# The first key tile and the rotation table brought and rotated in two parts, three small loads begun by another engine

## The chip, the cores and the metric

The kernel runs on one core of a Trainium2 chip. Its engines are TensorE (PE, with PEld for its weight loads), VectorE (DVE), ScalarE (ACT), GpSimd (POOL) and SyncE (SP), which here does nothing but issue transfers. Sixteen DMA engines move the data. The metric is the device time of one execution in microseconds (us): 590.54 us as the median of three runs before the change, 590.2 the fastest, 591.32 the slowest.

## The reference

Attention with rotary positions, then a two-layer perceptron with a squared ReLU. Batch 4, 8 heads, 576 positions, head size 64; the width is 512, the inner width 2048.

```python
def rotate(x):
    x1, x2 = x[..., :32], x[..., 32:]
    return concatenate([x1 * cos - x2 * sin, x1 * sin + x2 * cos], axis=-1)
scores = matmul(rotate(q), rotate(k).T) / 8
attn = exp(scores - max(scores)); attn = attn / (sum(attn) + 1e-9)
x = matmul(attn, v)                      # heads joined: 2304 x 512
r = maximum(x @ w_in, 0)
out = (s * (r * r) + b) @ w_out          # s and b are single numbers
```

## The kernel before

Heads are handled in 16 pairs; pairs 0 to 3 are the first batch. Of a pair, `st_k`, `st_q` and `st_v` hold 128 partitions by 9 (or 10) tiles of 64 numbers. Each k and q is loaded (L529), multiplied with the table and summed in three steps on DVE or POOL: `z` = x times the sines (L588), x = x times the cosines (L590), x = x + `z` (L592). For pairs 0 to 3, k and q are then turned by PE with the identity, four 128x128 transposes (L766) and two 64x64 pieces (L769), into one of two PSUM tiles named `s`; ACT copies the result into `qkT` (L412). From `qkT`, PE computes the scores of two row tiles at a time (L653) into both `s` tiles; DVE takes the row maxima `nm` (L678), and ACT the exponentials `p` (L412), after which the `s` tile is free again. Some of the `p` tiles are turned by PE with a diagonal matrix `dg` made from the identity (L794, L796).

Beside this, 32 blocks of the two weight matrices, 512 KB each, arrive as `x` (L440), are rebuilt by ACT (two passes, L412; POOL or DVE does some of them) and DVE (`wio<-x,wio`, L409), and PE forms a product of each with itself (L493) to find a bound of their size. From about 60 us the perceptron runs between the attention of later pairs, and PE has work of one kind or another to the end.

What every engine does next is written out: `plan` builds the list of pieces, `ORDER` says in which order they are emitted, `PICKS` which engine takes a piece that could go to several, `SLOTS` which buffer it uses. All loads go through SP's queue, in that order; an issue waits when its buffer or its completion semaphore (eight in turn) is not free. The rotation table `tab` (432 KB) is the first load, the identity `ident` (64 KB) the second, the k of pair 0 the third. The two scalars, `sb`, are loaded between the weights, and nine small DVE steps (`sb_scale`) use them later.

Of the kernel before, what the change touches and what calls it, by code (L numbers as in the profile page):

```python
# [42 lines left out]
    "BwKXEDJzEUJcJ0J2BYBxJ8EhKDJ9BdByBiKEBMBHCGCVCHKUKbJ-J1J_CIKAKFD8J3BNCbKGBjKeEIEVD9KcJqJ4B1KfALJ5KYKdEBJrKBK5B2KVKgJ6B3CX"
    "BzKhEQaaCWKiEHK6KHCKaZCYCcacD-CdB_K7abCeKlERCQB4KqadB5KjaeKZKrafKmakKsCLKkKtEKLfKIKaKnCAK8CMalLgKuFVCNELanKvCBEMC2ENKwb0"
    "LhEOamK9EPCCK-KxEEavB6aoLFapESCSKyEWKoCRLSEYayKJK0LGKpaqCTaxLHK1KCCOagC4EXC3CxawK_LTC5ahB8EZCgB7CJLCLULiCPEkLVB9LZEiKKLI"
    "LWLDaiKLKzLJLab1ajazb2b3K2LXLEarLjb4EqLKLra0Eab5a1Erb6asLkLLLsEjatLPL4CmLtElb7K3LMEtMFK4LbLNChCibGLQLAL5MGbJCzEmCjLBMHbI"
    "EnEuMIbHL6Llb8LYL7EoLoEsL_b9bKLOauCyEpEvEwbLLpLRa9bMEyLua8L8MAE6b-a7E5EzLvCra6b_FULqE7Exa2LwcAMJC0MOa-cBMKLxL9LcL1a_MUcC"
    "MLCoLybRMPEcL-MVL2bSE9cDMBbTMQLzE8bUFHL3cEFEMRbVcFL0bWbNFFcGFILnLea3LdcHMWE-CkMea4LmcICnMXMSMfCZMYCUbOEbcJMTCpa5MgcKE0MZ"
    "CfCtM0CaFGMbMhMlMCMiM1CsM6M2ClMjMrMEMaMDMcFXCDCuM7B-MkbeMsbACEbccLM8MtMMM9MmE_bPMuNBFAFhMNM3cMFBFJM-MnbdFCcNFDNCFMbfcOMd"
    "M4bBbgFKNEM5FTbCFNE1bXC6FibDNFM_EdC1NGNibhcPNfFYGINjMocQMvFLNkcRMwbENHNgNDcSNLMqMxNUMpbQNINANMNhbqNJFWMyEebpbiFeNVbnNlNN"  # L50
    "NmC7NWFjNRFfboNnNKNSCqNobrCvNvMzNTFgbYNwNqbZFOCwNxcaNrN9NXbscTbaGLNYN-cbNcNybtNOccNZNzcUN_cdNdGVOANPNecVbbdAOBcWbjFPN0ce"
    "dBbkNaN1FQcfdCblNbNQN2cXOCN6dDFZbmcYdEFRdFE2ODbudGOEdHFadIFbN3dJNsbvdKFcdLcZdMbwFdGWNpcgONdNFmbxE3FkchOQdPFnciFlbydOOFcj"
    "FoOOckdZdQN7dRcldYdSOGcmdTdidacndbFpN4djcoOPOROIFtPJcpdkNtbFPKcqOSE4dUOTPLOHOJdWFSPMdlOeN5dccrObNudVGXFqOKdsOUOcOYcsddOd"
    "d3N8ctOVOfcuFwd2GjOZdmFuFrOWOgdtF4d4FvdnOrd5bzOucvOhdeOiOscwOmdXOjOvOLcxOncydgOaPNOtF5dfOwOkdhOod6czO8OMdpc0O9duOXO5FxF6"
    "drdvc1eBOlPOO6c2O-eAGJc3dwGHPPc4PSdxOxeCeUd7O7Oyc5eVO2O_eDPAPTFyPEPVO3c6OpF7PBPWOzPFPUdoO4Oqdqc7PXdzPCPGc8eWdyO0PYeXPgF8"
    "PDGMFzd1Phd9F0FsPiO1PjF9eLeEPZPkPaF1QIPleFPdeKGKQJPmPeQLeMd_F2PnPbeNPrd0QMPHeOPsPoc9QNd8PtePQKd-F3PpF-c-P6PfeGQOGAP7eIPI"
    "c_PqP9ehF_eHP8GBGNeJPceQeieYQPejQTeSP-PQGmQwGOQQeZekeRPRP_eleTemGPenQRQAeaGCeoQBecQxQFebepGQQyeqGRederesGhQGetPxQZPyQCPu"
    "euPzGDGaQUewPwGSPvQHQaevQDQbQSGTQzQcefQlQVQ0P0exe5P1eyGUeeQEP2Qme6Q1P3GYfNezP4e7Qde0QeQ2QnQiP5fOe8QjQ3GbGiQ4e1GZfPG8e3Q7"
    "QfRKGcfDe9Q8Qke-fEfQQ5QoGEQpRLQtRBfFGFQqQWRMRCfGQufRQre_GlQ9RNRDGve2QhfSe4GwRbfHQsROfYGkREfIQYRPQ6fXGsRQRFGeGtRYQvQXRRGx"
    "fBRVRSRZfJfZQgfLRcRafARTfaG7fCG9RGGGegRsRdGnfiHxGoGpRWReGdG_RHfbfhGqGrRfRtG0Q-fjRjRgRkRuRhRpfkRXfKG-RqfMGuRJRrR6HGfsGyG4"  # L60
    "RIR7RAHAfrHJRvR8RlHKfTfcftRifVGzfuSVG1fURURwSWfdRxR0R3RySXG2ffR4fvHBfWR1feR5G5HCSYHDR9fwQ_fgHER-HFSKSZHVSCRmHwR_SLSaG3fl"
    "fmf2RnHHgCHIf1RogDHMSAfngEf3SBSDSHSbf4HLgFfpf5R2SIfoHOHzfqgGSJgHRzScfygIgJSdgKf6f0SMSEgLfxHPSNfzHSgMHNf7GfSggNgOf8SoHQgP"
    "f-f9ShgASlH0HWgQSmf_HvHYSegRSnGgG6SFgSSOSpgTSPgUgbSGSfHgSSHhSqS2HRgaSrSsSTSwSiS3Szgcg5StS0gdSUSQgegkHyHiSRHZgVg4S4H6HTHj"
    "S1glSxILS5HXS6TRS7gmTUTSS-gngWTVTTgXgZgfgoThS8g6Sjg7TiTWSuTXguHkS9TjS_IOTGTYHlTATZgvgpSkH9THSygYHUggTIH-SvTDHaghTEgwgiTa"
    "gxgqH_gyHbTtTFhMTuTcTJTKH7TOgjTLTkHcgrHdHeTqHfTlTdHoHmgtTrTvTBTMTmTPUJTCTbhNTsUKTwgzg8TNT4ULHphCT5TQUMg9T7hDTeTxT8TyT1g1"
    "hEIKT2g3TnT6g_HnhFgsT9Tzg0HqUVT-hGT_g2UWUATfhOUNhHUXUBhPUxUDT0INg-UETghAUyTohjUSH8hXhkUFUTUOhBhlUCUPhJhQhWUUhRTpIXUYUghY"
    "hmhIT3hnhZhLhoUZUhhaUdhTIjUahphqHrhKhbUihSUbUzgBhVhrhshtUjhuU0hvU1H1VIUkU2hdH2U3UlUGVJUmUeVZH3UIUnUcUrVKhUVahcUfH4hwVbVL"
    "heUHVcUsUoURU6hfImVMh7UtH5U7VNIAUph8ICUqVOU9VPVdh9VeiaU-UQh-VTHsVfiZIlh_IBU_hyVQIJU8VRHtibhxIuicVAIYVzIvhzUuV0hhh0VBhgh1"
    "VUVFWBU5iFUvWCVCU4IZUwV1iGIDWDVSVDViIMh2VwVEiQWEVxVGVyiPVViAiHVjiIVlVHiRh4IUV2h6VkWFVmIkIPiCIEV3WGV4iEIViSWNiJh3IWh5WHiB"
    "iKiTiDVniUiMIQV5WYVoiLIwVWIRIFWZISITV7IgWOiuIoV6VpV8VtWaVqiOInV9IciWIaVrWKWPVgitIxidIdIGVhWbiviNWciwiVVuWdiXIyVvijWLWeVs"  # L70
# [16 lines left out]
    "SSSSSSGSSSGGGVGGVGGVSGVGSSSSSGSSVVSSVVSSVVSSVVSSGSGSVGGSGVVGGSVVGSSGVSSSVGGSSGVSGSVVGGSVVSGSVVGSSVGSVSVVSGSVVSGSSGSSSSSG"  # L87
    "SGSVGSGSSSSSSSGSSSGSSGSSSGSGSSGVGGSSSSGSSSSSSGSSGSSSSSSSSSSGGSSSSSGVSSSSGSSSSSGSSGSSSSGVSGSSSSGSSGSGSVGSSSVSSSGSSGSSGSGG"
    "SGSSSSVGGSGGSGSSSGSSSGVSSVSVSSGSSVVGVSSVVGSGVVGSSVVVSSGVSSVVSSGVVVVVVGSSGVSSVGGSGVSVSVGGSGSVSSVSSSGVSGVVSGSSSSSSSSSSGSSS"
    "SSSGSSGSGSGSSSGSGGSGGSGGSSGSVSSSSSSSSSVSVSVSSSSVSSSSVVVSSSSSSSSSGSVSVSSSVSVSGSVVSVVVVSVSVVSVSVSSSSSSGSVVVVVVSSSVSVVVSSVV"  # L90
# [3 lines left out]
SLOTS = (
    "000111230101000001010102003011110011011011222130001310002013113020010103100110000101010011223012310100010101110112001121"
    "103011230030310011001334132500100100013001101031100103011003110514021013101021300130001132105200000111320114100310000121"
    "010001100320153112000310020110002111034100121041310113050011210000114200012331301002110103000031110233401012200001211021"
    "153011211110011032111201412211000320100520112110000113301202010200111310502001032011001300001011100011301140113020202121"
    "051020030002011110120121110003011120023501012001313014101111241000013020120101021225313201300011001030100110341200111310"
# [1001 lines left out]
```

## Time and profile before

| what | before |
|---|---|
| median of three runs | 590.54 us |
| the profiled execution | 591.62 us |
| its span from first to last instruction | 589.8 us |
| PE busy | 570.6 us, 97% of the span |
| DVE busy | 464.0 us, 79% |
| ACT busy | 417.1 us, 71% |
| POOL busy | 117.7 us, 20% |

The profiled execution is 1.82 us longer than its span: that much lies around the instructions. It is 1.08 us above the median of the runs. A row of a timeline gives the start, the duration, engine, line, operation, output from inputs, and in brackets the idle time of the engine before it and what ended it; rows of the same kind that follow each other are merged with a count.

### The profile page before, as it was taken

The numbers are of one execution on the slowest core, as the hardware profiler recorded it, in microseconds if no ns is written. First come the engines' busy times: TensorE is split into PE (matmuls) and PEld (weight loads), VectorE is DVE, ScalarE is ACT, GpSimd is POOL, SyncE is SP. The second block draws the span as 40 slices with busy tenths as digits, with TensorE's granted clock in tenths as the row PEclk, the third lists the DMA queues.
The fourth block names the chain that finished last, engine by engine and source line by source line (L and its number), as shares of the span: only waits on it lengthen the run. The fifth ranks groups of instructions, "written<-read, shape, count | busy, mean of one in ns | idle before, by whom it ended". The sixth has DMA issues, their size and how long they took to land.

```text
span 589.8 us, 12277 instructions
## 1 busy us (share of the span) xinstructions
PE 570.6 (97%) x4621; PEld 389.3 (66%) x4621; DVE 464.0 (79%) x975; ACT 417.1 (71%) x869; POOL 117.7 (20%) x123
## 2 busy tenths in 40 slices
...
PEclk9999999999999999999999999999999999999999
...
GB/s 300 345 299 297 243 256 214 191 184 151 155 203 156 122 180 169 222 193 185 168 105 167 186 147 148 151 169 143 101 102 21 82 93 84 57 61 1 37 1 36
DMA packets 210011, 90.32 MB, mean 153 GB/s; under 512 B 192288, under 2 KB 196768, under 8 KB 209952
## 3 DMA queue, kind: packets, MB, share of 16 engines
...
q14 instruction: 23, 0.19, 0.1%
...
## 4 chain that ended last, share of the span: by engine, by line
PE 91%; DVE 3%; DMA 2%; ACT 2%; issue 1%; SPq 0%; DVEq 0%
PE px L889 29%; PE po L972 27%; PE px L759 9%; PE s L671 8%; PE px L922 4%; PE po L943 4%; PE s L653 3%; PE s L972 2%; DMA st_k<-in_k_dram 2%; PE po L794 1%; PE s L672 1%; PE px L493 1%; PE px L813 1%; DMA pt<-pab 1%; PE s L660 1%
## 5 line engine op out<-in xcount | busy, mean ns | idle before, releaser
L889 PE MATMUL px<-xa,wio 128*128 128x256 f16 x1536 | 179.7, 273 | 0.0
L972 PE MATMUL po<-wio,g 128*128 128x512 f16 x720 | 171.4, 379 | 0.8 <-ACT o L412 0.8
L889 PEld LDWEIGHTS <-wio 128*128 128x128 f16 x1536 | 147.7, 98 | 28.6 <-issue 2.0
L412 ACT ACTIVATE p<-s,nm 128x576 f32<-128x576 f32 x144 | 105.4, 733 | 36.0 <-DVE s L680 23.1
L972 PEld LDWEIGHTS <-g 128*128 128x128 f16 x816 | 75.8, 98 | 74.0 <-issue 3.4
L409 DVE SCALAR_TENSOR_TENSOR pab<-p,sum,pab 128x576 f16<-128x576 f32 x136 | 114.0, 849 | 7.6 <-ACT pab L412 3.7
L680 DVE TENSOR_SCALAR_CACHE_REDUCE s<-s,sc 128x576 f32<-128x576 f32 x108 | 87.9, 818 | 16.8 <-PE s L672 15.7
L406 POOL TENSOR_SCALAR pab<-p,sum 128x576 f16<-128x576 f32 x54 | 48.1, 894 | 240.5 <-DVE sum L708 189.7
L412 ACT ACTIVATE hr<-px,xc 128x512 f32<-128x512 f32 x64 | 43.7, 682 | 52.4 <-PE px L889 52.3
L913 DVE SCALAR_TENSOR_TENSOR g<-hr,xc,g 128x512 f16<-128x512 f32 x64 | 48.4, 761 | 18.8 <-ACT g L412 18.1
L412 ACT ACTIVATE pab<-p,sum 128x576 f16<-128x576 f32 x64 | 48.7, 767 | 11.0 <-DVE sum L708 10.4
L404 DVE TENSOR_SCALAR g<-hr,xc 128x512 f16<-128x512 f32 x24 | 11.9, 497 | 47.9 <-ACT hr L412 32.6
L759 PE MATMUL px<-pt,v 128*64 128x320 f16 (+2 forms) x640 | 48.9, 281 | 0.3 <-DMA pt<-pab 0.2
L412 ACT ACTIVATE hr<-hr 128x512 f32<-128x512 f32 x68 | 42.7, 628 | 1.5
L671 PE MATMUL s<-qkT 128*128 128x512 f16 (+1 forms) x120 | 41.4, 383 | 0.1
L671 PE MATMUL s<-kS,qkT 128*128 128x512 f16 (+1 forms) x120 | 41.3, 380 | 0.0
L412 ACT ACTIVATE g<-hr,xc 128x512 f16<-128x512 f32 x40 | 28.7, 717 | 16.9 <-PE po L972 10.9
L759 PEld LDWEIGHTS <-v 128*64 128x64 f16 x640 | 32.1, 110 | 11.1 <-issue 7.4
L671 PEld LDWEIGHTS <-qkT 128*128 128x128 f16 (+1 forms) x240 | 22.5, 100 | 22.8 <-issue 3.7
L922 PE MATMUL px<-x,wio 128*128 128x128 f32 x256 | 31.4, 278 | 0.0
L922 PEld LDWEIGHTS px<-x,wio 128*128 128x128 f32 x256 | 29.8, 192 | 2.2 <-issue 1.2
L412 ACT ACTIVATION_READ_ACCUMULATOR p<-s,nm 128x1 f32 x144 | 28.2, 196 | 0.0
(154 smaller groups left out, 796.3 us busy)
## 6 DMA issues: line engine op xcount, KB each, us to landing
...
```

The costliest lines, as they stand in the source:

```text
L406: eng.tensor_scalar(out=out, in0=in0, scalar1=s1, scalar2=s2, op0=op0, op1=op1)
L409: nc.vector.scalar_tensor_tensor(out=out, in0=in0, scalar=scalar, in1=in1, op0=op0, op1=op1)
L412: nc.scalar.activation(out=out, in_=in_, func=func, **kw)
L653: nc.tensor.matmul(ps[h][:, to], d["qF"][hh, t * P:(t + 1) * P], d["kF"][hh, keys], start=True, stop=True)
L671: nc.tensor.matmul(ps[rows, MAIN:2 * MAIN], lhs, kk[:, h:8:2], start=(n == 0), stop=(n == 1))
L680: nc.vector.tensor_scalar(out=T["s"], in0=T["s"], scalar1=st[pr]["es"], scalar2=None, op0=ALU.mult, op1=ALU.min, accum_out=T["nm"])
L759: nc.tensor.matmul(o[64 * h:64 * h + 64, c], v_rows(pr, h, k, z), p_rows(pr, 2 * (i // 4) + h)[:, k, c], start=((z, k) == todo[0]), stop=( ...
L889: nc.tensor.matmul(ph, w16[0][:, f, wz, cc], X["xa"][:, xz, c], start=(c == 0 and n == 0), stop=(c == NC - 1 and n == 2))
L913: nc.vector.scalar_tensor_tensor(out=g[:, 1], in0=r, scalar=xs[u]["c"][:, 2:3], in1=g[:, 0], op0=ALU.add, op1=ALU.subtract)
L922: nc.tensor.matmul(ph, wi[:, f + 1, c * P:(c + 1) * P], xs[0]["x"][:, c, j * P:(j + 1) * P], start=(c == 0), stop=(c == NC - 1))
L943: nc.tensor.matmul(X["po"][:, j * DM:(j + 1) * DM], gs["h", j, f - f % 4][:, f % 4 * P:(f % 4 + 1) * P], wo[:, f + 1], start=(n == 1), sto ...
L972: nc.tensor.matmul(po, g[:, gz, jj], w16[1][:, f, wz, to], start=(n == 1 and i == 0), stop=(n == NF and i == 2))
```

## The change

The table is loaded in two parts, tiles 0 to 3 and tiles 4 to 8, and so is the k of pair 0; the loads alternate (table, k, table, k) at the head of SP's queue. The rotation of that k runs as two pieces of three steps each, one for each part, and the first part is given to POOL. The identity and the two scalars are no longer pieces of the plan: ACT's queue issues them before its first instruction. The order, the engines of many pieces and the buffers are written out anew for the whole program.

```diff
 ORDER = (
-    "AAC8C9A9AMDYDZAXAyDADBDDDCA_DEDGA-DFANBADIDKAODcA4DHAPBBDJDdAiI9DLDfDMAYDeAZI-A0AaAzDgAnI_A1JFJADiARA5DOA6DhJGDmA7AkDkJB"
+    "AAC7ABC8C9A8DbALDcAWAxDADBDDDCDEDGDFDHA9DJA-DIDfDLDKDNA_ANDgA3DMDODiAMDPJADhAXAOAYJBAhJIAzAyAZJJDjAaAQJCDlA0JDA4DkAmA5DR"
...
         for nm in "kqv":
-            add(DMA, "load_x", pr, nm, w=[(nm, pr)])
+            if pr == 0 and nm == "k":
+                for i in range(2):
+                    add(DMA, "load_h", pr, nm, i, p=[(nm, pr)], w=[("half", i)])
+            else:
+                add(DMA, "load_x", pr, nm, w=[(nm, pr)])
...
         for nm in "kq":
-            add((DVE, POOL), "rotate", pr, nm, steps=3, r=[("tab",)], w=[(nm, pr), ("z", pr, nm)])
+            if pr == 0 and nm == "k":
+                for i in range(2):
+                    add((DVE, POOL), "rot_half", pr, nm, i, steps=3, r=[("tab", i)], w=[("half", i)], p=[(nm, pr), ("z", pr, nm)])
+            else:
+                add((DVE, POOL), "rotate", pr, nm, steps=3, r=[("tab", 0), ("tab", 1)], w=[(nm, pr), ("z", pr, nm)])
...
-    add(DMA, "load_tab", w=[("tab",)])
     for i in range(2):
-        add(DMA, "load_sb", i, p=[("sb",)])
-    add(DVE, "sb_scale", steps=9, r=[("sb",)], w=[("sc0",)])
+        add(DMA, "load_tab", i, w=[("tab", i)])
+    add(DVE, "sb_scale", steps=9, w=[("sc0",)])
...
-    def load_tab():
-        nc.sync.dma_start(out=tab, in_=rope)
-        nc.sync.dma_start(out=ident, in_=eye)
...
+    def cut(i):
+        return slice(4 * i, 4 + 5 * i)
+
+    def load_h(pr, nm, i):
+        if not i:
+            st[pr][nm] = new(stage, nm, [P, 9, D], F32, "st_" + nm)
+        nc.sync.dma_start(out=st[pr][nm][:, cut(i)], in_=src_of[nm][pr][:, cut(i)])
+
+    def load_tab(i):
+        nc.sync.dma_start(out=tab[:, cut(i)], in_=rope[:, cut(i)])
...
+    nc.scalar.dma_start(out=ident, in_=eye)
+    for i in range(2):
+        nc.scalar.dma_start(out=sb[:, i:i + 1], in_=(s, b)[i].partition_broadcast(P))
     nc.vector.memset(ones32, 1.0)
```

Three places where the order moves. The first is the head of SP's queue. Before (`x` is a weight block; `st_k_117` and `st_q_119` are the k and q of pair 2):

```order
L532 DMA tab<-in_rope_dram 128x864
L533 DMA ident<-in_eye_dram 128x128
L529 DMA st_k_109<-in_k_dram 128x576
L529 DMA st_q_111<-in_q_dram 128x576
L440 DMA x_113<-in_moe_w_in_dram 128x1024
L440 DMA x_115<-in_moe_w_in_dram 128x1024
L529 DMA st_k_117<-in_k_dram 128x576
L529 DMA st_q_119<-in_q_dram 128x576
```

Now:

```order
L547 DMA tab<-in_rope_dram 128x384
L544 DMA st_k_111<-in_k_dram 128x256
L547 DMA tab<-in_rope_dram 128x480
L544 DMA st_k_111<-in_k_dram 128x320
L536 DMA st_q_115<-in_q_dram 128x576
L447 DMA x_117<-in_moe_w_in_dram 128x1024
L536 DMA st_k_119<-in_k_dram 128x576
L447 DMA x_121<-in_moe_w_in_dram 128x1024
```

The last part of pair 0's k is now the fourth issue and its q the fifth, where they were third and fourth; the first weight block moved from fifth to sixth.

The second is the rotation of pair 0 at the head of DVE. Before:

```order
L588 TENSOR_TENSOR z_125<-st_k_109,tab 128x9x2x32
L590 TENSOR_TENSOR st_k_109<-st_k_109,tab 128x576
L588 TENSOR_TENSOR z_128<-st_q_111,tab 128x9x2x32
L592 TENSOR_TENSOR st_k_109<-st_k_109,z_125 128x576
L590 TENSOR_TENSOR st_q_111<-st_q_111,tab 128x576
L592 TENSOR_TENSOR st_q_111<-st_q_111,z_128 128x576
```

Now on DVE:

```order
L607 TENSOR_TENSOR z_129<-st_k_111,tab 128x5x2x32
L609 TENSOR_TENSOR st_k_111<-st_k_111,tab 128x320
L607 TENSOR_TENSOR z_135<-st_q_115,tab 128x9x2x32
L611 TENSOR_TENSOR st_k_111<-st_k_111,z_129 128x320
L609 TENSOR_TENSOR st_q_115<-st_q_115,tab 128x576
L611 TENSOR_TENSOR st_q_115<-st_q_115,z_135 128x576
```

And at the head of POOL, behind one set-up instruction that stood there before the change as well:

```order
L607 ISA
L607 TENSOR_TENSOR z_129<-st_k_111,tab 128x4x2x32
L609 TENSOR_TENSOR st_k_111<-st_k_111,tab 128x256
L611 TENSOR_TENSOR st_k_111<-st_k_111,z_129 128x256
L413 TENSOR_SCALAR wio<-x_127 128x512
```

DVE keeps five of nine tiles of that k; POOL has the other four as its first work.

The third is DVE at the first two row maxima. Before (`st_q_119` is the q of pair 2, `z_210` belongs to the k of pair 1):

```order
L678 TENSOR_REDUCE nm_185<-s_170 128x1
L409 SCALAR_TENSOR_TENSOR wio<-x_121,wio 128x512
L590 TENSOR_TENSOR st_q_119<-st_q_119,tab 128x576
L409 SCALAR_TENSOR_TENSOR wio<-x_123,wio 128x512
L678 TENSOR_REDUCE nm_197<-s_171 128x1
L588 TENSOR_TENSOR z_210<-st_k_151,tab 128x9x2x32
L592 TENSOR_TENSOR st_q_119<-st_q_119,z_178 128x576
```

Now (`st_q_123` is the q of pair 2):

```order
L697 TENSOR_REDUCE nm_185<-s_175 128x1
L697 TENSOR_REDUCE nm_189<-s_176 128x1
L416 SCALAR_TENSOR_TENSOR wio<-x_125,wio 128x512
L609 TENSOR_TENSOR st_q_123<-st_q_123,tab 128x576
L416 SCALAR_TENSOR_TENSOR wio<-x_127,wio 128x512
L611 TENSOR_TENSOR st_q_123<-st_q_123,z_170 128x576
L607 TENSOR_TENSOR z_222<-st_k_160,tab 128x9x2x32
```

The second maximum moved up by three places, and the last step of pair 2's q by one. Elsewhere in the same stretch, the diagonal `dg` of pair 0's first turned tile is now made by ACT, between the two copies into `qkT` of pair 2, where POOL made it.

## Rows read from the trace of the kernel before

**Rows 1.** The page: the span, and TensorE's granted clock in 40 slices.

```profile
span 589.8 us, 12277 instructions
...
PEclk9999999999999999999999999999999999999999
```

**Rows 2.** Stretches: length, busy time by engine, granted clock, DMA share, GB/s.

```profile
20.00:30.00 10.00, 9.81 (x73) 7.49 (x74) 9.82 (x19) 7.86 (x16) 1.92 (x2) 1.00 1.00 372
30.00:40.00 10.00, 8.62 (x91) 6.79 (x89) 9.68 (x24) 8.36 (x16) 3.79 (x6) 1.00 0.93 313
80.00:160.00 80.00, 79.21 (x592) 52.04 (x589) 78.18 (x161) 71.08 (x154) 23.50 (x23) 1.00 0.89 191
160.00:480.00 320.00, 319.92 (x2638) 213.22 (x2636) 282.26 (x610) 240.19 (x511) 66.74 (x67) 1.00 0.65 144
480.00:560.00 80.00, 79.22 (x604) 54.53 (x602) 25.63 (x51) 32.75 (x55) 2.56 (x3) 1.00 0.26 61
```

**Rows 3.** PE's waits over the span: us in total, times, longest.

```profile
PE s L766 <- DVE st_k L592: 9.3, 1, 9.3
PE s L766 <- ACT p L412: 3.2, 2, 1.7
```

**Rows 4.** Timeline of the first 16 us.

```profile
0.73 1.28 ACT L412 ACT_TABLE_LOAD   x1 [0.73 <-PEq L1078]
0.74 0.39 SPq L532 DMA_DIRECT2D tab<-in_rope_dram  x1
...
1.65 0.43 SPq L529 DMA_DIRECT2D st_k<-in_k_dram  x1
2.12 0.43 SPq L529 DMA_DIRECT2D st_q<-in_q_dram  x1
...
6.36 0.76 DVE L588 TENSOR_TENSOR z<-st_k,tab 128x576 f32<-128x576 f32 x1 [5.22 <-DMA st_k<-in_k_dram]
...
8.31 0.67 ACT L412 ACTIVATE x<-x 128x512 f32<-128x512 f32 x1 [6.30 <-DMA x<-in_moe_w_in_dram]
...
9.30 1.12 PE L766 MATMUL s<-ident,st_k 128*128 128x128 f32 x4 [9.30 <-DVE st_k L592]
9.95 0.76 DVE L592 TENSOR_TENSOR st_q<-st_q,z 128x576 f32<-128x576 f32 x1
...
10.76 1.11 PE L766 MATMUL s<-ident,st_q 128*128 128x128 f32 x4
...
13.04 2.40 PE L653 MATMUL s<-qkT 64*128 64x512 f32 x8 [0.21 <-ACT qkT L412]
...
15.47 0.76 DVE L678 TENSOR_REDUCE nm<-s 128x1 f32<-128x576 f32 x1 [0.88 <-PE s L653]
```

**Rows 5.** Timeline from 15 to 27 us.

```profile
17.14 1.12 PE L766 MATMUL s<-ident,st_k 128*128 128x128 f32 x4 [1.71 <-ACT p L412]
...
18.01 0.75 DVE L678 TENSOR_REDUCE nm<-s 128x1 f32<-128x576 f32 x1
...
19.34 0.75 DVE L592 TENSOR_TENSOR st_q<-st_q,z 128x576 f32<-128x576 f32 x1
...
20.19 1.09 PE L766 MATMUL s<-ident,st_q 128*128 128x128 f32 x4 [1.52 <-ACT p L412]
20.61 0.15 DVE L708 RECIPROCAL sum<-sum 128x1 f32<-128x1 f32 x1
...
20.87 0.79 POOL L406 TENSOR_SCALAR dg<-ident,sum 128x128 f32<-128x128 f32 x1 [20.43 <-DVE sum L708]
...
24.61 1.11 PE L766 MATMUL s<-ident,st_q 128*128 128x128 f32 x4
...
26.07 0.72 PE L766 MATMUL s<-ident,st_k 128*128 128x128 f32 x4
```

**Rows 6.** What reads the table, on POOL: ns min/median/max, first and last start.

```profile
L588 POOL TENSOR_TENSOR z<-st_q,tab x3: 1417/1842/1902, 47.7 to 293.4; 128x576 f32<-128x576 f32 x3
```

**Rows 7.** The page's transfers: the table, us from issue to landing.

```profile
tab<-in_rope_dram SPq DMA_DIRECT2D x1, 432.0 KB, 3.4
```

**Rows 8.** Timeline of 14 to 45 us: a scalar's issue.

```profile
28.61 2.93 SPq L536 DMA_DIRECT2D sb<-in_moe_s_dram  x1
```

More of the change, by code (lines that the diff above doesn't have):

```diff
@@ L43 @@
[L43 to L70, printed above, removed]
@@ new lines @@
+    "JfEjJ2BwBREKEXJ_BWBvJ3KGKACFBXBxBLKHBcBhKXBGCaCGKeAHJ4CHKBD_J6KCAICUBiKDBMELKhEAEYKIKfJtJ7KJEEKiJ8KYJuAJKEB1KgB0K8AKKbJ9"
+    "CbB2ByaeCcETCJKjCVKkadCdKlCWK9B-afKKCXK-acEUCPKoEBB3KtagB4KmK_ahKcENKuKpaoKvKnLAKLCLLBLiKdKwKqElEOCKanLjKxB_EkCMCAapCQLk"
+    "EPC1EQaqCBCRERLILlEVB5KyarESb3LCasEZKrKzLVK3a0EbLJKFK0CSKsa1aiEaKMLWazK4C3ajK1E8C2CwCIEtLKakC4B6CNEcayLXCfB7COLFEua2B8a3"
+    "KNLmLYLGatLZEmLLb4alK2Lcb5LaamLMb6EwK5auLHEHEnavEdb7LdLNCxLuExCyb8a4awLOLvClb9KOLPL7axLnLwEvK6Chb-MILQK7LbLSLoEoL8bLLeEp"
@@ new lines @@
+    "MJL9E_bJEyLRbKEqL-Czb_LTMKbMLEErMCEscALrMLbNFHLUcBEza-LsbOCgLxLDa9L_cCLybAMAEecDa_FILtE9E0bVbBCqMME-CiMRbCcELzMNL0LfL1L4"
+    "MXcFCmMSE1L2bUFAMBcGL5bWcHL3E2MYa5cIMTbXLpFKMZcJa6MDLgL6MObYa7bPcKMULqLhFLbZFBMaa8MeMhMEcLMVCrCTCYCjCZCeMWE3FJbQMiCkMfbh"
+    "CnMjFMM3MbFWMkcMFXCsMlMFbaM4cNM9M5McbDMuMgCtMoCoMHbgMGMpM-MdCCMvEfB9biCDMqM_cOMwFCbfNAFDMmNEMQM6MxFEcPNFFaFFcQbEMnNBFGNH"
+    "cRbFFPM7MPFNNIbGFQM8bRcSGLbjEgFkNlNJcTbSNCbkFYNKFlbsblE4MyNmNLNiMzMrNjNONncUNPcVNXNGNMFTbHMtFOMsbtNDFbEhFZbqM0NQNkFhC0NY"
@@ new lines @@
+    "C5bTGOC6FmNNNoNZNUFiCuNpNVCpNqbbM2CvNWNrNyFjbcM1NaNzNtOAcdNbN0brFRNfOBNcbdcWbuNdN1cXbvbeN2bwceNRcYN3cfNgcZFScgNuODNTGYNS"
+    "bmFUdDOEbnchE5dEFcbocidFbIcaE6N4dGOCbpdHFddIOFGmN5bxdJdKFeNsdLFfcbdMbydNdOGZdPbzccFwb0dQNvcjN6OQckOTdSOGNhclOHN7b1FgcmdR"
+    "FpFnNeORcndcdTFqdUcodbOLFocpOMdmFrddcqFzOUdlcrdedVFVOSNwGaOVcsdWPMctNxN8OedfPNdvOIcuFsdnOJcvdYN9ONOfdaPON-dwdoOKOWdpcwOh"
+    "OXdxdgObd6N_FtOiOgOcdiGMcxPPd5dqOjcyOYOxE7dXczOkPQFyOZdydZd7OlOuOyOpOOd8F7Omc0GpeEOnc1OaOzOvdzeDc2OoOwOqc3F1O_OdPRdkPAeF"
```

95 lines of the change are left out of this document (57 added, 38 removed).

## The prediction

> **What bounds the kernel now.** I read the page first, then busy time by stretch, then PE's waits, then the timeline of the first 27 us. TensorE bounds it: from 40 us to 560 us it stands for 1.65 us in all (0.79 in 80 to 160 us, 0.08 in 160 to 480, 0.78 in 480 to 560) [rows 2], and its work there is the same in both kernels. So the end can move in three ways only: PE starts earlier, PE stands less in the first 40 us, or PE's work runs for a shorter time at a low clock.
>
> The first wait is the largest, 9.3 us for the rotated k [rows 3]. In it, DVE begins at 6.36 when k has landed, six steps start 0.72 us apart up to 9.95, and PE's first transposes start at 9.30, when k's third step is done [rows 4]. Two more waits, 3.2 us together, stand before the transposes at 17.14 and 20.19: the two score tiles are taken, until DVE has found their maxima (15.47 and 18.01) and ACT has read them [rows 3, 5]. From 20 to 40 us DVE is busy for 9.82 and 9.68 of each 10 us, and PE stands 0.19 and 1.38 us [rows 2]: DVE is nearly the bound there.
>
> Four transposes take 1.12 us at 9.30 and 17.14, 1.09 at 20.19, 1.11 at 24.61, and 0.72 at 26.07 [rows 4, 5]. The page grants the full clock in every slice [rows 1], but these durations say 1.2 GHz to about 26 us and 2.4 GHz after; before the rise PE had worked since 20.19 with no wait of note. A wait taken away before the rise therefore counts once, by what it shifts the rest.
>
> **The change part by part.** *Loads.* When the last part of k lands, the table, the identity and k have been asked for in both kernels, 784 KB; only the order inside has changed. SP's issues stand 0.47 us apart (1.65 to 2.12) [rows 4], so the last part of k is issued at 2.1 instead of 1.65 and q at 2.6 instead of 2.12. If the bytes set the landing, DVE starts at 6.36 as now; if the issue sets it, at 6.83; if ACT's three issues also push SP's aside, at 0.43 us each, at 8.1. I take 6.36, since 784 KB in about four microseconds is what the engines moved, and keep 5.9 (identity on a way of its own) to 8.1.
>
> *First half on POOL.* It needs 384 KB (192 of table, 128 of k, 64 of identity), less than the 432 KB of table that landed 3.4 us after its issue, at 4.1 [rows 7]. POOL takes 1.42 to 1.90 us for a step of 576 columns [rows 6], by proportion 0.63 to 0.85 for 256; three are 1.9 to 2.6, done at 6.0 to 6.7. It is wanted at about 8.4 (below), so 1.7 us or more are to spare, and PE does its two transposes (0.56) meanwhile.
>
> *Second half on DVE.* A step of 576 columns takes 0.75; the smallest DVE instruction 0.15 [rows 5]. So 320 columns take 0.15 + 0.60 x 320/576 = 0.48 (between 0.42 and 0.75). Three of k's are cheaper by 0.27 each, 0.8 us together: k is done at about 8.4, q at 9.9 where it was 10.71. PE's k is then ready by 9.5, q's transposes begin at 9.9 instead of 10.76, and the scores at 12.2 instead of 13.04 [rows 4]. Lead: 0.85 us.
>
> *Maxima side by side.* Between the end of the scores and the last step of pair 2's q DVE had seven instructions (two maxima, two joins of weights, the q's second step, a step of pair 1's k, the q's third); now six, the step of the k standing behind. That is 0.7 less before the q, but ACT's exponentials gate the transposes too. After the scores' end at 14.6: maxima to 16.1, three instructions and the last step to 18.9. So q's transposes start at 18.9 instead of 20.19: lead 1.3 us for PE. The k of pair 2 must wait for the first exponential and comes at 17.05, near the 17.14 of before, but it is not what ends the stretch. DVE's own lead is smaller, since a step was only put behind: 0.8 us less work on it, and 0.4 less standing at 15.47, minus what the shorter pieces lose: I take 0.8.
>
> *Identity and scalars on ACT.* Three issues at 0.4 us put the table load (1.28) back to about 2.0 to 3.3; a scalar's issue took 2.93 once on SP [rows 8], then it would be 5.9. ACT's first work is at 8.31 [rows 4]: hidden by 2.4 us either way. SP is freed of that 2.93 us at 28.6, in a stretch in which DVE was busy 98%: I price it at nothing, with an upper end of 0.3 gained.
>
> *The rest of the order.* Same instructions but for a few that changed engines. What it can give is the 1.38 us that PE stands in 30 to 40 us, or lose a like amount.
>
> *Sum.* PE leads by 1.3 us at 18.9 us; in the 20 us behind it, DVE, with 0.8, is the nearer bound. Between the two I take 1.0. On the profiled execution: 591.62 - 1.0 = 590.6. That execution is 1.08 us above the median of the runs, so 590.54 - 1.0 = **589.5 us**.
>
> POOL's first work today starts at 20.87, 0.1 us after DVE's reciprocal that it waits for (20.61 plus 0.15) [rows 5], and nothing in the trace shows when POOL could have begun at the earliest. The Trainium skill, "GPSIMD Engine Reference", section 2.1 Instruction dispatch, says that the first call to a freshly loaded kernel pays a code load of about 6 us that no instruction of the profile shows. At 20.87 the trace does not agree, as no such gap stands there; only a load that runs right behind the set-up instruction at the start would fit both, and as an estimate by that page POOL would begin at 6.7 us.
>
> **Rivals.** *POOL begins late.* Its three steps then run beside DVE's, at 0.63 to 0.85 each; if it begins when DVE does (6.4) or later, the half is done at 8.3 to 9.2, and all of k's transposes (1.55) come behind: q's start at 9.9 to 10.8, so a lead of 0.85 to 0, with the 0.4 of the maxima kept: 589.7 to 590.3, say 590.1. For: nothing proves POOL ready earlier; against: its first work today started at once. Chance 0.08.
>
> *The second half lands late*, because it is a later issue or because two queues share the way: 0.47 to 1.7 us at DVE's start against the 0.85 and the 0.4 gained. Time 589.8 to 591.0, say 590.4. For: no row shows two queues side by side; against: the bytes ahead are the same. Chance 0.16.
>
> *The waits of 30 to 40 us go too.* DVE has less to do early and SP no longer stands 2.93 us: PE's whole 1.3 is kept and its 1.38 us of standing halves to vanishes. 590.54 - 1.3 - 1.0 = 588.2. Chance 0.18.
>
> *Slower: the low clock lasts longer.* [...] Chance 0.13.
>
> **How the numbers follow.** Forecast 0.45, its own range 588.9 to 590.1. A measurement tells from no change what exceeds 0.2%, that is 1.18 us: below 589.36 is faster, above 591.72 slower. Of the forecast's 0.45, 0.21 lie below 589.36; with 0.18 of the third rival and 0.01 of the others, 0.40 for faster. Slower is 0.12 of the fourth rival and 0.03 for a second half that lands at the far end together with new waits: 0.15. The rest, 0.45, is no change. The range that holds 8 in 10 runs from 587.9 to 591.8: it takes in the first three rivals and the nearer part of the fourth.
>
> **What would show it.** Right: POOL's three steps in 4 to 7 us; DVE's first step near 6.4 and its q done near 9.9; scores from 12.2; pair 2's q transposed from 18.9; four transposes falling to 0.6 or 0.7 near 25; idle of PE in the first 40 us of about 13 us instead of 14.1. Wrong: DVE's first step after 7, POOL's first after 6, a wait of PE between 19 and 25 us, or new waits of PE after 40 us beyond the 1.65.

## The result, and the profile after

The changed kernel takes 593.68 us (median of 5 runs, 592.88 to 594.42) against 590.54: ratio 1.0051, 95% interval 1.0039 to 1.0063. It is slower by 3 us and lies above the predicted range. The profiled execution took 593.68 us too; its span is 591.9 us, 2.1 above that of before [rows 1]. The medians lie 3.1 apart, since the profiled execution of before was 1.08 above its median; the two traces can account for 2.1.

The first views are the stretches at the start and later (length, busy time by engine, granted clock, DMA share, GB/s).

```profile
2.00:3.00 1.00, 0.00 (x0) 0.00 (x0) 0.00 (x0) 0.87 (x1) 0.00 (x0) 1.00 0.90 262
3.00:4.00 1.00, 0.00 (x0) 0.00 (x0) 0.00 (x0) 0.42 (x1) 0.00 (x0) 1.00 0.35 71
4.00:5.00 1.00, 0.00 (x0) 0.00 (x0) 0.00 (x0) 0.00 (x0) 0.00 (x0) 1.00 0.26 55
5.00:6.00 1.00, 0.00 (x0) 0.00 (x0) 0.00 (x0) 0.00 (x0) 0.91 (x2) 1.00 0.48 133
...
0.00:40.00 40.00, 25.38 (x192) 18.23 (x193) 30.90 (x60) 26.33 (x49) 7.75 (x15) 1.00 0.86 312
80.00:160.00 80.00, 78.86 (x586) 51.70 (x585) 76.57 (x162) 71.25 (x154) 19.84 (x21) 1.00 0.92 193
160.00:480.00 320.00, 317.67 (x2624) 212.69 (x2622) 280.27 (x599) 241.94 (x512) 66.54 (x63) 1.00 0.68 146
480.00:560.00 80.00, 80.00 (x603) 54.19 (x602) 34.00 (x71) 30.44 (x50) 0.76 (x1) 1.00 0.23 54
```

Two things differ from before. The transfers all but stop: 71 and 55 GB/s from 3 to 5 us, in the very microseconds in which the first k and the table should land. And PE stands 2.33 us between 160 and 480 us, where it stood 0.08; the 0.78 us of 480 to 560 us are gone [rows 2]. Before, the first 40 us were:

```profile
0.00:40.00 40.00, 25.88 (x197) 18.82 (x197) 32.50 (x62) 26.89 (x49) 5.91 (x12) 1.00 0.92 320
```

So PE stands 14.62 us in the first 40 us, 0.50 more than before and 1.6 more than the 13 that I had forecast. Behind them it stands 1.82 us more (0.35 more in 80 to 160 us, 2.25 more in 160 to 480, 0.78 less in 480 to 560). Against the kernel before, most of the loss that the trace shows is the middle's.

PE's waits over the span say what for (us in total, times, longest).

```profile
PE s L785 <- POOL st_k L611: 7.4, 1, 7.4
PE px L500 <- DVE wio L416: 2.6, 2, 2.1
PE s L785 <- DVE st_k L611: 2.4, 1, 2.4
PE s L690 <- ACT p L419: 2.2, 3, 1.2
```

The 9.3 of [rows 3] has become 7.4 + 2.4; the two waits for a free score tile (3.2) are gone, and 2.6 us for joined weights are there instead. The last row is the new loss of the middle. The timeline of the start shows the same by instruction.

```profile
5.01 0.72 POOL L607 TENSOR_TENSOR z<-st_k,tab 128x256 f32<-128x256 f32 x1 [4.57 <-DMA st_k<-in_k_dram]
...
7.39 0.69 PE L785 MATMUL s<-ident,st_k 128*128 128x128 f32 x2 [7.39 <-POOL st_k L611]
...
8.31 0.49 DVE L607 TENSOR_TENSOR z<-st_k,tab 128x320 f32<-128x320 f32 x1 [7.18 <-DMA st_k<-in_k_dram]
...
14.20 2.40 PE L672 MATMUL s<-qkT 64*128 64x512 f32 x8 [0.75 <-ACT qkT L419]
...
19.11 1.05 PE L785 MATMUL s<-ident,st_k 128*128 128x128 f32 x4
...
20.68 1.09 PE L785 MATMUL s<-ident,st_q 128*128 128x128 f32 x4
...
26.02 0.78 PE L785 MATMUL s<-ident,st_q 128*128 128x128 f32 x4
```

DVE begins at 8.31 instead of 6.36 and the scores at 14.20 instead of 13.04 [rows 4]; the q of pair 2 follows its k by 1.57 us instead of 3.05, so that it is only 0.49 late at 20.68 [rows 5]. The page's transfers (KB, us from issue to landing) name the late ones: the second parts take 6 us, and so do 512 bytes of a scalar.

```profile
tab<-in_rope_dram SPq DMA_DIRECT2D x1, 240.0 KB, 6.1
tab<-in_rope_dram SPq DMA_DIRECT2D x1, 192.0 KB, 2.7
...
st_k<-in_k_dram SPq DMA_DIRECT2D x1, 160.0 KB, 6.0
st_k<-in_k_dram SPq DMA_DIRECT2D x1, 128.0 KB, 3.7
ident<-in_eye_dram ACTq DMA_DIRECT2D x1, 64.0 KB, 2.6
sb<-in_moe_s_dram ACTq DMA_DIRECT2D x1, 0.5 KB, 3.4
sb<-in_moe_b_dram ACTq DMA_DIRECT2D x1, 0.5 KB, 6.0
```

The middle has its own cause. The timeline of the changed kernel from 189 to 199 us, DVE's, POOL's and the last two links:

```profile
190.78 3.42 DVE L416 SCALAR_TENSOR_TENSOR pab<-p,sum,pab 128x576 f16<-128x576 f32 x3
190.94 1.91 POOL L607 TENSOR_TENSOR z<-st_q,tab 128x576 f32<-128x576 f32 x1
...
193.73 1.74 POOL L609 TENSOR_TENSOR st_q<-st_q,tab 128x576 f32<-128x576 f32 x1 [0.87 <-ACT junk L419]
...
194.12 1.96 DVE L611 TENSOR_TENSOR st_k<-st_k,z 128x576 f32<-128x576 f32 x1
...
196.00 0.81 DVE L699 TENSOR_SCALAR_CACHE_REDUCE s<-s,sc 128x576 f32<-128x576 f32 x1
...
196.97 0.74 ACT L419 ACTIVATE p<-s,nm 128x576 f32<-128x576 f32 x1 [2.41 <-DVE s L699]
...
197.85 0.38 PE L690 MATMUL s<-qkT 128*128 128x512 f16 x1 [1.22 <-ACT p L419]
```

Read it backwards: PE waits 1.22 us for the exponential that frees a score tile, ACT waited 2.41 us for the maximum of L699, and DVE came to that late because its own rotation step took 1.96 us, where one takes 0.75 alone. Three joins of `pab` took 3.42, where the run m3 below shows 2.27. Each long DVE instruction lies beside a rotation step of POOL. At 232 to 237 us it happens again: two DVE instructions of 1.95 us beside two POOL steps, and PE waits 0.22 and 0.74 us at 239 and 240 us.

### The profile page after: what moved, and what is told of

Read it like the earlier page. It is cut to its first block, busy times and chain, and to the rows that moved or that the text cites. A ratio compares the mean times of both kernels' runs of the same rounds, so it can differ in the third digit from the quotient of the medians.

```text
span 591.9 us, 12283 instructions
## 1 busy us (share of the span) xinstructions
PE 570.5 (96%) x4621; PEld 389.1 (66%) x4621; DVE 467.8 (79%) x989; ACT 415.6 (70%) x863; POOL 113.0 (19%) x118
## 5 line engine op out<-in xcount | busy, mean ns | idle before, releaser
L699 DVE TENSOR_SCALAR_CACHE_REDUCE s<-s,sc 128x576 f32<-128x576 f32 x108 | 87.4, 818 | 16.1 <-PE s L691 14.9
L413 POOL TENSOR_SCALAR pab<-p,sum 128x576 f16<-128x576 f32 x48 | 44.8, 937 | 242.7 <-DVE sum L727 172.7
L932 DVE SCALAR_TENSOR_TENSOR g<-hr,xc,g 128x512 f16<-128x512 f32 x64 | 50.0, 789 | 21.2 <-ACT g L419 20.9
L419 ACT ACTIVATE pab<-p,sum 128x576 f16<-128x576 f32 x71 | 53.7, 765 | 7.7 <-DVE sum L727 4.2
L411 DVE TENSOR_SCALAR g<-hr,xc 128x512 f16<-128x512 f32 x22 | 10.6, 483 | 36.1 <-ACT hr L419 22.8
L690 PEld LDWEIGHTS <-qkT 128*128 128x128 f16 (+1 forms) x240 | 22.5, 100 | 23.9 <-issue 5.0
L419 ACT ACTIVATE g<-hr,xc 128x512 f16<-128x512 f32 x42 | 30.0, 715 | 10.3 <-PE po L991 7.0
L691 PEld LDWEIGHTS <-qkT 128*128 128x128 f16 (+1 forms) x240 | 22.0, 100 | 9.4 <-issue 5.2
```

Source lines behind the costliest of these rows:

```text
L411: eng.tensor_scalar(out=out, in0=in0, scalar1=s1, scalar2=None, op0=op0)
L413: eng.tensor_scalar(out=out, in0=in0, scalar1=s1, scalar2=s2, op0=op0, op1=op1)
L419: nc.scalar.activation(out=out, in_=in_, func=func, **kw)
L690: nc.tensor.matmul(ps[rows, MAIN:2 * MAIN], lhs, kk[:, h:8:2], start=(n == 0), stop=(n == 1))
L691: nc.tensor.matmul(ps[rows, MAIN - TAIL:MAIN], lhs, kk[:, 8, 64 * h:64 * h + 64], start=(n == 0), stop=(n == 1))
L699: nc.vector.tensor_scalar(out=T["s"], in0=T["s"], scalar1=st[pr]["es"], scalar2=None, op0=ALU.mult, op1=ALU.min, accum_out=T["nm"])
```

## The experiments

All ratios are to the kernel before, run on the same chip; its median there was 590.68 to 591.13 us. The four groups of runs (e1, e2, e3 and h1; m2, x1, x3 and b1; c1 to c3; m3) come from different chips, so runs of different groups are compared by these ratios, which can differ by up to 0.07% from the quotient of the medians. The brackets are 95% intervals; two runs are called told apart where their intervals lie apart.

**e1: scalars back at their place.**

```diff
-    for i in range(2):
-        nc.scalar.dma_start(out=sb[:, i:i + 1], in_=(s, b)[i].partition_broadcast(P))
...
+            if x["fn"] == "load_w" and a == (1, 0):
+                for i in (1, 0):
+                    nc.sync.dma_start(out=sb[:, i:i + 1], in_=(s, b)[i].partition_broadcast(P))
```

> The changed kernel, but the two scalars are loaded by SP's queue at the place they had before the change (ahead of the weight block that came behind them); the identity stays on ACT's queue, halves and order stay. Scalars (their 256 reads of four bytes held back the halves, 71 and 55 GB/s in 3 to 5 us): DVE starts at 6.2 to 6.6 instead of 8.31, PE's scores at about 12.3 instead of 14.20, and if the lateness also made the 2.2 us of PE waits at 198 to 240 us, the time is 589 to 590. New order (the waits of 198 to 240 us belong to the order): DVE early as above, but these waits stay within 0.5 us, time 591 to 592. Halves or two queues (short rows or ACT's queue are what is slow): DVE still starts after 7.5, time 593 to 594.

Measured: 592.74 us, 1.0038 (1.0021 to 1.0054). From 3 to 6 us the transfers move 203, 202 and 351 GB/s; POOL begins at 3.95, DVE at 6.64, the scores at 12.73. The waits of 2.2 us for `p` stay. The scores now start before the old kernel's 13.04 [rows 4], yet the run is 0.38% slower than that kernel: there is a second cause. The time lies above the 591 to 592 expected for this case, and its interval overlaps the changed kernel's, so the 0.9 us between the two medians are not told from nothing. In the trace, PE also stands 1.27 us in 30 to 40 us, behind the scalars' old place (0.64 in the changed kernel), and 0.8 us for a transposing transfer.

**e2: the old kernel, with identity and scalars first on ACT's queue.**

```diff
-        nc.sync.dma_start(out=ident, in_=eye)
...
+    nc.scalar.dma_start(out=ident, in_=eye)
+    for i in range(2):
+        nc.scalar.dma_start(out=sb[:, i:i + 1], in_=(s, b)[i].partition_broadcast(P))
```

> The kernel before, with one part of the change alone: the identity and the two scalars issued by ACT's queue ahead of its first instruction; order, whole table and whole k as before. Scalars: the dip of the DMA rate to under 150 GB/s appears before 6 us, k's first step moves from 6.36 to 7.8 to 8.5, the time rises by 1.5 to 2.5 to about 592.5. New order or halves: the start stays within 0.4 us of 6.36 and the time at 590 to 591.

Measured: 591.91 us, 1.0021 (1.0012 to 1.0030). Not k falls into the stall, as I had expected (7.8 to 8.5), but q: k comes before it (DVE at 5.65 instead of 6.36), and then the transfers move 188, 58 and 160 GB/s from 4 to 7 us. DVE waits 1.47 us for q, and the scores start at 13.89. No wait stands in the middle. This edit alone costs 1.2 us, less than the 1.5 to 2.5 expected.

**e3: one number per partition from 128 places.**

```diff
-        nc.scalar.dma_start(out=sb[:, i:i + 1], in_=(s, b)[i].partition_broadcast(P))
+        nc.scalar.dma_start(out=sb[:, i:i + 1], in_=rope[:, 1, i:i + 1])
```

> The changed kernel, with the two small loads reading one number per partition from 128 different rows of the table (3456 bytes apart) instead of one number 128 times; same places, sizes and queue. It leaves out the right values of s and b. One address (128 reads of the same four bytes stand in line): the dip goes, DVE starts at 6.2 to 6.8, time as in the run with the scalars at their old place. Smallness (any 256 reads of four bytes do it): dip and start at 8.3 stay, time 593 to 594.

Measured: 591.82 us, 1.0018 (1.0009 to 1.0027). The stretches of e3:

```profile
3.00:4.00 1.00, 0.00 (x0) 0.00 (x0) 0.00 (x0) 0.41 (x1) 0.00 (x0) 1.00 0.87 213
4.00:5.00 1.00, 0.00 (x0) 0.00 (x0) 0.00 (x0) 0.00 (x0) 0.72 (x1) 1.00 0.81 163
```

The same 256 reads of 4 bytes, on the same queue at the same time, but from 128 places each: 213 and 163 GB/s in place of 71 and 55, DVE at 6.68, scores at 12.58, and PE stands 13.0 us in the first 40 us instead of 14.62. Its interval lies apart from the changed kernel's. So it is not that the reads are small; what matters is that 128 of them ask for one address. Whether 128 addresses close to each other would do the same is not tested: here they lie 3456 bytes apart.

**h1: halves in the old order, scalars at their old place** (the old order with the half pieces set in at its head).

> The order, engines and buffers of the kernel before, with the halves put in at the head (table, k, table, k; first half rotated by POOL, second by DVE), the identity on ACT's queue, the scalars at their old place. If the halves do what was predicted: DVE starts near 6.4, q done near 9.9, scores at 12.2, and with the old order's 1.65 us of PE waits after 40 us the time is 589.3 to 590. If the old order can't use an earlier start: 590.3 to 590.8. New order as the cause of the loss at 198 to 240 us: none of those waits here.

Measured: 591.16 us, 1.0001 (0.9992 to 1.0010). q is rotated 0.6 us earlier than before, but the scores start at 13.11, as before: ACT's first work waits for its weights until 9.51 (8.31 before [rows 4]), its copies of q stand behind that work, and PE waits 0.88 us for them. No waits stand in the middle. The halves alone, loaded in four parts, give nothing in the old order.

**m2: identity and both scalars as one load.**

```diff
-    nc.scalar.dma_start(out=ident, in_=eye)
-    for i in range(2):
-        nc.scalar.dma_start(out=sb[:, i:i + 1], in_=(s, b)[i].partition_broadcast(P))
+    nc.scalar.dma_start(out=idsb, in_=eye)
```

> The changed kernel, but s and b stand as two more columns of rows behind the identity (130 columns instead of 128, laid out ahead), so that one load on ScalarE's queue brings all three and no number is read 128 times. Theory (the broadcast reads cost the start, the new order costs the middle): PE's first transposes near 6.3 us instead of 7.4, scores near 12.6 instead of 14.2, the 2.2 us of waits of s for p between 190 and 245 us stay, 591.8 us (591.3 to 592.3). Rival (the load on ScalarE's queue in itself delays the table): start as in the changed kernel, 593.5. Rival (the new order is sound, and its waits come from the late start): the 2.2 us are gone, 589.5.

Measured: 592.8 us, 1.0036 (1.0022 to 1.0050); its profiled execution took 595.1. Scores at 13.33, since q came 0.64 late; the 2.3 us of waits for `p` stay. In time it lies between the first two theories, but the waits are where the first put them. Its interval overlaps the changed kernel's.

**x1: only the head in the new order** (ORDER up to piece 640 of the changed kernel, then the old sequence; loads as m2).

> As m2, but only the first 640 pieces (to about 115 us) stand in the new order, all others in the order of the kernel before; seven buffers are chosen anew for that. Theory (the new order gains about 0.9 us at the head and loses 2.2 between 190 and 245 us): no waits of s for p there, PE stands under 0.3 us from 160 to 480 us, 589.7 us (589.3 to 590.3). Rival (the lead of the head is not kept, whatever follows): waits of 0.7 us or more come between 115 and 300 us, 590.6 or more. Rival (the waits come from the head's buffers): the 2.2 us stay, 591.8.

Measured: 591.0 us, 1.0007 (0.9997 to 1.0016). The stretch of x1 that lost before:

```profile
160.00:480.00 320.00, 320.00 (x2640) 213.34 (x2638) 282.32 (x611) 240.62 (x512) 68.55 (x67) 1.00 0.64 144
```

PE never stands there: the waits belong to what the new order does after 115 us. But the 0.9 us that I had given the head are not there: 591.0, not 589.7. In this profile q came late again, and the scores started at 13.06, as before; even so PE stood 13.48 us in the first 40 us, 0.64 less than before. The first rival, that the lead isn't kept, has both its signs: 590.6 or more, and one wait of over 0.7 us. Here is that wait, in the kernel before and then in x1, with DVE's instruction that delays it in the kernel before (beside POOL's rotation steps of 134.93 and 136.75):

```profile
135.32 2.03 DVE L409 SCALAR_TENSOR_TENSOR v<-st_v,sc,v 128x640 f16<-128x640 f32 x1
138.41 0.62 PE L493 MATMUL px<-wio 128*128 128x128 bf16 x8 [0.42 <-DVE wmx L496]
```

```profile
138.51 0.62 PE L444 MATMUL px<-wio 128*128 128x128 bf16 x8 [0.98 <-DVE wmx L447]
```

PE is ready 0.46 us earlier (137.53 against 137.99) and goes on 0.10 later, because DVE, whose `v` starts at 135.43 here, is no earlier than before. What was left of the head's lead on PE ends there.

**x3: as x1, with the new order again from 385 us on.**

> As x1, and from piece 2026 on (about 385 us) again the new order. Theory: what the new order gains behind 480 us, 0.78 us of a wait of po for o, comes on top of the head: 588.9 us (588.5 to 589.5). Rival (that gain is only the slack which the middle's loss left): as x1, 589.7.

Measured: 590.39 us, 0.9993 (0.9983 to 1.0004): 0.6 below x1, near the wait of 0.78 us that has gone at 480 to 560 us, though the two intervals overlap. The total is higher than expected, as x1's: the wait at 138 us stands here too (until 138.73).

**b1: the old kernel with m2's one load**, nothing in halves.

> The kernel before with its own order and whole loads; the identity, s and b come in one load of 130 columns as ScalarE's first issue, and SP issues no scalar any more. Theory: the 64 KB of the identity run beside the table, q lands as before, SP's 2.9 us at 28.6 and the dip of the transfers at 32 to 34 us are gone, but no wait of PE hung on them: 590.4 us (589.9 to 590.8), PE's first transposes 9.1 to 9.4. Rival (the stall at 28.6 us held back weights that PE waited for in 30 to 40 us): the 1.4 us of waits there shrink by half, 589.8. Rival (a second queue delays k or q): 591.0 or more.

Measured: 590.18 us, 0.9989 (0.9980 to 0.9998). Without the identity in front of it on its queue and without a stall, k lands for DVE to begin at 5.17, not 6.36, and the scores start at 12.10, earlier than in any kernel with halves. That is more than the theory asked for (9.1 to 9.4 for the first transposes; they came at 8.36). PE still stands 1.31 us in 30 to 40 us, 1.38 before [rows 2], so its waits there did not hang on the stall. From e2 this run differs only in how identity and scalars are loaded: the ratios lie 0.32% apart (1.9 us), with intervals apart. That is the price of the broadcast reads in the old order.

**c1: x3 with the first table and k as whole loads**, only the work in halves.

```diff
-        nc.sync.dma_start(out=st[pr][nm][:, cut(i)], in_=src_of[nm][pr][:, cut(i)])
+            nc.sync.dma_start(out=st[pr][nm], in_=src_of[nm][pr])
...
-        nc.sync.dma_start(out=tab[:, cut(i)], in_=rope[:, cut(i)])
+        if not i:
+            nc.sync.dma_start(out=tab, in_=rope)
```

> As x3, but the table and the first k come as whole loads (table, then k); only the work is in halves, first half on GpSimd, second on VectorE. Theory (the four smaller loads land later than two whole ones: k at 5.2 us in b1, its second half at 5.6 to 6.7 here): VectorE's first step at 5.2 us instead of 6.7, GpSimd's too (instead of 3.9), PE's first transposes at 7.4, the q rotated by 8.5, scores near 11.8 instead of 13.2, 589.4 us (588.8 to 590.0). Rival (the start of the scores is not what the end hangs on): scores earlier, time as x3, 590.4. Rival (the late landing comes from the second queue or the order, not from the split): VectorE begins at 6.4 or later, 590.4 or more.

Measured: 589.9 us, 0.9982 (0.9966 to 0.9999). Its interval overlaps x3's. DVE begins at 5.32 instead of x3's 6.71: with the split loads it begins later. Of the 1.4 us, 0.97 is the later issue of the last part (at 2.15 in x3, the whole k at 1.18 here); the rest is a longer way from issue to landing (4.5 us against 3.9). The forecast of scores near 11.8 failed (12.66), and the timeline of c1 shows why.

```profile
5.32 0.49 DVE L552 TENSOR_TENSOR z<-st_k,tab 128x320 f32<-128x320 f32 x1 [4.18 <-DMA st_k<-in_k_dram]
5.36 1.03 POOL L552 TENSOR_TENSOR z<-st_k,tab 128x256 f32<-128x256 f32 x1 [4.92 <-DMA st_k<-in_k_dram]
5.84 0.89 DVE L554 TENSOR_TENSOR st_k<-st_k,tab 128x320 f32<-128x320 f32 x1
6.47 0.85 POOL L554 TENSOR_TENSOR st_k<-st_k,tab 128x256 f32<-128x256 f32 x1
6.66 1.27 DVE L552 TENSOR_TENSOR z<-st_q,tab 128x576 f32<-128x576 f32 x1
7.40 1.12 POOL L556 TENSOR_TENSOR st_k<-st_k,z 128x256 f32<-128x256 f32 x1
7.86 1.01 DVE L556 TENSOR_TENSOR st_k<-st_k,z 128x320 f32<-128x320 f32 x1
```

Started together, DVE's and POOL's steps lengthen each other: DVE's 0.49 becomes 0.89 and 1.01, its 0.76 becomes 1.27, POOL's 0.72 becomes 0.85 to 1.12. Little is gained by working at the same time.

**c2: b1 with the new order from 385 us on.**

> As b1 (order of the kernel before, whole loads, one load for identity and scalars), but from piece 2026 on (about 385 us) the new order. Theory (the new order's end is worth what x3 was faster than x1, 0.6, the wait of po for o behind 480 us): that wait of 0.78 is gone and the time is 589.5 us (589.0 to 590.0). Rival (x3's gain over x1 was chance or the wait only moves): 590.2.

Measured: 589.26 us, 0.9982 (0.9966 to 0.9998); the wait of 0.78 us is gone (PE busy 80.00 of 80 us from 480 to 560). Its median is the lowest of all, and it beats both kernels, the one before by 0.18% with an interval that just excludes no change. Its interval overlaps b1's, so what the new end adds is not told from nothing.

**c3: c2 with the first k's work in halves.**

> As c2, but the first k is rotated in halves, the first on GpSimd (loads whole). Theory (in the old order the scores stand behind a sum over weights and the copies, so VectorE's 0.8 us are not passed on): scores at 12.0 to 12.3 as in b1, 589.5 us, same as c2. Rival (VectorE is the near bound of 20 to 40 us and its 0.8 us count): 588.9.

Measured: 590.06 us, 0.9984 (0.9969 to 0.9998). It is not told apart from c2, and DVE's and POOL's steps lengthen each other as in c1 (DVE's 0.89, 1.27 and 1.02 us). The scores start at 12.68, later than the 12.0 to 12.3 expected. The rival's 588.9 did not come.

**m3: m2 without six of POOL's rotation steps.**

```diff
     def rotate(pr, nm, e):
+        if (pr, nm) in ((8, "q"), (10, "q")):
+            return
```

> As m2 (the changed order, one load), but the rotation of q of pairs 8 and 10 is left out: six steps of GpSimd, at 192 to 199 and 234 to 244 us in m2; those two q stay unrotated. Nothing of VectorE's, ScalarE's or PE's work changes. Theory (GpSimd's tensor_tensor steps and VectorE's instructions slow each other: VectorE's took 1.95 and 1.96 us there, 0.75 to 0.81 alone, and its maxima come late for ScalarE's exponentials and so for PE): VectorE's instructions there take 0.7 to 0.85 each, PE's waits of s for p (2.3 us) fall under 0.5, and the time falls by about 2 us against m2, to 590.8 (590.3 to 591.3). Rival (the new order has simply put too much before the maxima on VectorE): instructions may be shorter but 1.5 us or more of the waits stay, 592.3 or more. Rival (VectorE's long instructions have another cause): they stay at 1.9 us.

Measured: 590.42 us, 0.9995 (0.9982 to 1.0009), 2.4 below m2, with intervals apart. DVE in m3, at the place shown above for the changed kernel:

```profile
188.97 2.27 DVE L416 SCALAR_TENSOR_TENSOR pab<-p,sum,pab 128x576 f16<-128x576 f32 x3
191.15 0.75 DVE L613 TENSOR_TENSOR st_k<-st_k,z 128x576 f32<-128x576 f32 x1
191.82 0.81 DVE L701 TENSOR_SCALAR_CACHE_REDUCE s<-s,sc 128x576 f32<-128x576 f32 x1
```

And the first engines' row of the page, of m2 and then of m3:

```profile
PE 571.9 (96%) x4621; PEld 390.4 (66%) x4621; DVE 468.5 (79%) x989; ACT 415.9 (70%) x863; POOL 113.5 (19%) x118
```

```profile
PE 570.5 (97%) x4621; PEld 389.8 (66%) x4621; DVE 462.9 (79%) x989; ACT 416.2 (71%) x863; POOL 104.2 (18%) x112
```

The same 989 instructions of DVE take 5.6 us less, since six of POOL's are gone. All three waits at their old places are gone. Half the expectation failed: one wait of 1.37 us stands at 242 us, where ACT waits 2.68 us for a transposing transfer; PE comes to this place 4.8 us earlier than in the changed kernel. PE in 160 to 480 us, m2 and then m3:

```profile
160.00:480.00 320.00, 317.55 (x2630) 213.28 (x2629) 281.74 (x601) 242.94 (x513) 66.79 (x63) 1.00 0.68 145
160.00:480.00 320.00, 318.51 (x2631) 213.09 (x2630) 274.98 (x601) 243.91 (x515) 57.26 (x57) 1.00 0.69 148
```

So the traces show 1.0 us for the edit (PE stands 1.49 us instead of 2.45), not the 2 expected, and not all of the 2.4 us is the middle's. Before the first step that is left out, PE already stands 1.1 us less in the first 40 us (the scores start at 12.21, 1.1 before m2's, as q did not come late) and 0.9 less in 80 to 160 us. The two heads are the same, so this is the difference of two executions; m2's profiled one lay 2.3 us above its median.

## Why the prediction was wrong

*Loads, and "identity and scalars on ACT".* This step failed first. I bounded DVE's start by bytes and by issues (5.9 to 8.1, I took 6.36) and priced the scalars by ACT's issue time alone, "hidden by 2.4 us either way". The issues were as forecast, 0.40, 0.46 and 0.45 us, and ACT's table load ended at 3.41, harmless. The cost lay where I had no term: what the 256 reads do to the other transfers. DVE began at 8.31, beyond the upper bound. Taken out of the changed kernel, this is worth 1.9 us with intervals apart (e3, where PE stands the forecast 13.0 us in the first 40 us), and 0.9 by the medians of e1 and m2, which are not told apart from the changed kernel. In the old order it costs 1.9 us (e2 against b1). The 6.36 itself rested on the bytes: b1 asks for as many and DVE begins at 5.17, so the bytes alone do not set it. The trace of before had it: here are the stretches of the old kernel right after the scalars' issue [rows 8] had ended at 31.5 us.

```profile
31.00:32.00 1.00, 0.52 (x7) 0.53 (x8) 1.00 (x2) 1.00 (x3) 0.00 (x0) 1.00 0.91 345
32.00:33.00 1.00, 0.65 (x9) 0.43 (x8) 1.00 (x4) 0.94 (x4) 0.00 (x0) 1.00 0.86 154
33.00:34.00 1.00, 1.00 (x19) 1.00 (x19) 0.97 (x2) 1.00 (x3) 0.00 (x0) 1.00 0.58 116
34.00:35.00 1.00, 0.80 (x9) 0.49 (x6) 1.00 (x4) 0.29 (x1) 0.00 (x0) 1.00 0.95 373
```

I read from [rows 8] that an issue takes 2.93 us, and not what the transfers do behind it. Moving that load moved a stall from a place where no wait of PE hung on it (b1) to the place where everything waits for transfers.

*"The rest of the order"*, priced at plus or minus 1.38 and placed in 30 to 40 us. This step failed by its place, and the sum had it at nothing: the loss is 2.2 us of waits between 190 and 245 us (x1 against m2: 1.7 us of time), since the new order lays POOL's rotations of two q beside DVE's work right before maxima that ACT and PE wait for. m3 shows that these POOL steps lengthen DVE's instructions and make these three waits, though its trace gives back 1.0 us of PE's standing and not 2.2. I said that PE's work after 40 us is the same, which is true, and took its idle time to be the same, which does not follow. The sign stood in [rows 6]: one step of 576 columns took 1417, 1842 or 1902 ns, and I used the spread only as a range. In the old kernel DVE's `pab` and `v` took up to 1.97 and 2.03 us beside POOL too. At most of these places PE did not wait, but behind the 2.03 stands its wait of 0.42 us at 138.41 (shown at x1).

A page of the Trainium skill would have warned me: "SBUF — State Buffer", section "SBUF: two separate sides", says that VectorE and GpSimd share one pair of ports, which goes to one instruction for its whole length, for a VectorE instruction with two inputs in SBUF against a GpSimd one that reads SBUF; the other stands still. The traces agree with it: 1.96 us against 0.75, and the lengthened steps of c1.

*First half on POOL.* Right. Its steps take 0.72 us (0.63 to 0.85 forecast), and it begins as soon as its data have landed, at 5.01 here and 3.95 in e1. The late start at 6.7 us is seen in no run: where POOL has a half, it begins at 3.88 to 5.38. The 6.7 was an estimate from the code load of about 6 us at a first call that the Trainium skill states, "GPSIMD Engine Reference", section 2.1 Instruction dispatch.

*Second half on DVE.* The step is 0.49 us (0.48 forecast), but the second half of k lands later than a whole k could: with split loads DVE begins at 6.3 to 6.8 us in all kernels without the stall, with whole loads and the identity on its own queue at 5.2 to 5.7 (b1, c1, c2, c3). This lateness is more than the three shorter steps give (0.8). About 1.0 us of it is the later issue of the last part (c1 against x3). Why four loads also take longer to land than two of the same bytes stays open: the rate at 4 to 5 us is 143 to 206 GB/s in all kernels with split loads and without the stall, and 391 in c1.

*Maxima side by side.* The lead was there: the q of pair 2 follows its k by 1.57 us instead of 3.05, and 1.16 us of delay at the scores had become 0.49 at that q. A new wait stands in its place, 2.11 us for joined weights at 18.70.

*Sum.* I let 1.0 us of lead run on to the end, the part that DVE, as the nearer bound, was to carry. x1 shows that DVE does not carry it: behind the same head it starts its `v` at 135.43 instead of 135.32, and PE, 0.46 us ahead, waits for it at 138.51. With the new order behind 115 us this wait does not stand, and the waits of the middle come instead.

*The slower rival*, the low clock lasting longer, was on the right side with the wrong mechanism: four transposes took 1.09 us at 20.68 and 0.78 at 26.02, where before they took 1.11 at 24.61 and 0.72 at 26.07 [rows 5]. The durations fall at about the same time, though PE waited 0.46 us for joined weights at 22.64. What a longer low clock would have cost, as part of the range's upper end and of the chance for slower, no run shows; the loss came from the stall and the middle. *"The second half lands late"* was the right mechanism at the start, with 0.47 to 1.7 us for DVE (it was 1.95) and for the most part the wrong reason: without the broadcast reads DVE begins at 6.68 (e3), 0.3 late, and the other 1.6 us are theirs.

The sum, by the runs: the changed kernel is 0.51% slower. Without the broadcast reads 0.33 of it goes by e3 and 0.15 by m2; from m2, the old order from 115 us on takes off 0.29 (x1). What is left in x1, 0.07, is not told from nothing. The shares come from different kernels and need not add up. The steps that were to gain, halves and maxima, gave nothing that can be measured in the time (h1, x1); against b1, which has the one load and whole pieces in the old order, x1 is 0.18% slower, and the two intervals just touch.
